# Fourier transform and gated feed-forward on one core: loads of mu behind x, tables of k1 = 0 derived later, padded weights, a short mix in one operation, a late table load

## The chip, the cores and the metric

One core of one Trainium2 chip runs the whole program. The metric is the device time of one execution in microseconds (us). A run's trace is one execution; its span, from the first to the last instruction, is about 2 us shorter than that execution's time (459.5 against 461.36 us for the kernel before). Engines are named as in the profile: PE is TensorE (matmuls), PEld its weight loads, DVE VectorE, ACT ScalarE, POOL GpSimd, SP SyncE.

## The reference

For x of 8 batches, 3072 positions and 256 features, in float32:

```python
X = np.fft.fft(np.fft.fft(x, axis=1), axis=2).real          # the real part of both transforms
x_prev = X shifted by one position (zeros in front)
xk = mu_k * X + (1 - mu_k) * x_prev
xr = mu_r * X + (1 - mu_r) * x_prev
k = relu(xk @ w_k)                                           # 256 -> 1024
out = sigmoid(xr @ w_r) * ((k * k) @ w_v)                    # 1024 -> 256
```

## The kernel before

The transform over positions is done in steps: x is multiplied with twiddles `w_pm` (96 rows), then the features are transformed with `w_eo` ("d products", into `g_all`), then 64-column matmuls with the sine tables `m1` and `m2` make the second position step ("c items", into `pq`). VectorE makes sums and differences of neighbours (`halves`, `diff`), mixes them by mu (`scaled`, `mixed`), and the k, r and v products follow. Everything is spread over one list of steps; from step 0 on, k products of one chunk run with v products of a former one. The parts that matter here:

```python
def m_rest(part):                       # after the sine and its swap, on VectorE
    s = 26 if part else 0
    if not part:                        # four 64x64 tables for feature 128
        V.tensor_copy(out=cs[lo64, 0], in_=m1[lo64, 1])
        V.tensor_copy(out=cs[hi64, 0], in_=m2[hi64, 1])
        ...                             # two more
    for m in (m1, m2):
        V.tensor_scalar(out=m[hi64, s], in0=m[hi64, s], scalar1=-1.0, ...)
        ...
            V.memset(m[hi64, 1], 0.0)
            V.tensor_copy(out=tw[:, 0 if m is m1 else 1, 0:1], in_=m[:, 0, 0:1])

def c_item(b, s0, n, eng="A"):
    ...
    if b and s0 + n == NSL:             # feature 128, once in each of batches 1 to 7
        for k in range(2):
            nc.tensor.matmul(out=ps[0:NSL, 448:512], lhsT=y_t[b, "u"][:, k],   # 27 columns
                             rhs=cs[:, k], start=(k == 0), stop=(k == 1))
    evac(pq..., eng)                    # "A": ScalarE, "V": VectorE

def v_out(c, tb, n):
    o = o_pool.tile([P, 2, 256], FP32, name="o")        # three buffers in a ring
    ...                                                 # one operation on VectorE, then two stores
        eng = nc.scalar if s and n == 1 else nc.sync

loads()                                 # SyncE: six loads of mu; GpSimd: gathers of the weights
a_sum(0, 0, 0)
a_sum(0, 0, 4)
m_sine(0, NS1)
...
m_sine(NS1, NSL)
nc.scalar.activation(out=pd_f, in_=m_pi, func=AF.Sigmoid)     # loads the sigmoid's table early
d_item(0, 3)
for lo, hi in ((0, 4), (4, 8)):         # the first two pieces of the first mixed x
    halves(0, lo + (lo > 0), hi + 1)
    diff(0, lo, hi)
    for a in range(2):
        scaled(0, 0, 0, a, lo, hi)
        mixed(0, 0, 0, a, lo, hi)
...
at(3, c_item, 0, 17, 8, "V")
```

## Time and profile before

| | before |
|---|---|
| time, median of 3 runs | 463.28 us (463.28 to 463.38) |
| the profiled execution | 461.36 us, span 459.5 |
| TensorE busy, share of the span | 450.2 us, 98% |
| first d product (record of TensorE) | 16.75 us |
| eighth group of k products starts | 38.77 us |
| from there to the end of the span | 420.7 us |

The last two rows are the ones to keep in mind. From the eighth group of k products on, the chain of waits of the kernel before has only TensorE pieces, up to the last outputs, so an execution is "when does that group start" plus "how long is the rest". (Here and below the start is that of the group's first matmul record. The chain's figure, 38.93 in the prediction, is 0.16 more, since the chain counts a piece only from the end of the one before.) The second row has a catch that I saw only later: the profiled execution was 1.9 us faster than any of the three timed ones.

### The profile page before, as it was taken

What the parts mean: (1) busy time and instruction counts of PE and PEld (TensorE: products, weight loads), DVE (VectorE), ACT (ScalarE), POOL (GpSimd) and SP (SyncE); (2) the same over time, 40 slices, a digit from 0 to 9 for tenths busy, and PEclk for the clock granted to TensorE, in tenths of its full rate; (3) what the DMA queues carried; (4) which work ended last, traced back from release to release, by engine and by line L of the source; (5) the groups of instructions that cost most, each with busy time, mean ns of one, the idle gap of its engine ahead of it and who ended that gap; (6) DMA issues with size and microseconds to landing.
All of it is one profiled execution on the core that took longest, in us unless ns stands there. A gap on an engine that the chain in (4) does not pass through costs nothing.

```text
span 459.5 us, 9810 instructions
## 1 busy us (share of the span) xinstructions
PE 450.2 (98%) x4089; PEld 329.2 (72%) x4089; DVE 361.6 (79%) x533; ACT 357.9 (78%) x397; POOL 34.9 (8%) x67
## 2 busy tenths in 40 slices
PE   8889999999999999999999999999999999999996
PEld 4657777777777777777777777777777777676765
DVE  7899978987788777978688777888679855898443
ACT  3898898788878887888878888878887888666662
POOL 8821000001000000000000000000000000000000
PEclk9999999999999999999999999999999999999999
DMA  7995462625623373324722265222222232323324
GB/s 120 147 170 100 110 137 47 139 66 119 139 47 71 56 150 95 70 58 91 165 56 65 52 138 118 69 51 66 58 60 61 56 70 47 71 59 80 70 66 95
DMA packets 32972, 40.25 MB, mean 88 GB/s; under 512 B 4480, under 2 KB 30592, under 8 KB 31584
## 3 DMA queue, kind: packets, MB, share of 16 engines
q1 hardware_dynamic: 28080, 25.07, 22.8%
q0 software_dynamic: 4688, 14.42, 18.6%
q8 instruction: 32, 0.52, 0.5%
q10 hardware_dynamic: 160, 0.13, 0.1%
q14 instruction: 12, 0.10, 0.1%
HBM read 28.84 MB, written 25.17 MB: 118 GB/s over the span
## 4 chain that ended last, share of the span: by engine, by line
PE 92%; DVE 4%; DMA 2%; issue 1%; ACT 0%; POOL 0%; SPq 0%; DVEq 0%; POOLq 0%
PE psV L573 36%; PE psW L536 35%; PE psW L559 9%; PE psW L422 4%; PE psW L398 4%; PE psW L449 3%; PE psW L412 1%; DMA xh<-in_x_dram 1%; DVE t L501 1%; DVE x L514 1%; DMA out_dram<-o 1%; DVE y L481 0%; DVE d L489 0%; DVE a L384 0%; DVE pq L384 0%
## 5 line engine op out<-in xcount | busy, mean ns | idle before, releaser
L546 ACT ACTIVATE rl<-psW 128x1024 f16<-128x1024 f32 x192 | 196.7, 1025 | 83.6 <-PE psW L536 83.6
L536 PE MATMUL psW<-x,wk 128*128 128x512 f16 (+1 forms) x776 | 197.4, 377 | 1.6 <-DVE x L514 1.3
L573 PE MATMUL psV<-wv_sb,k 128*128 128x256 f16 x1536 | 198.7, 273 | 0.0
L552 DVE TENSOR_TENSOR k<-rl 128x2048 f16<-128x2048 f16 x96 | 117.4, 1223 | 62.5 <-ACT rl L546 61.9
L573 PEld LDWEIGHTS <-k 128*128 128x128 f16 x1536 | 143.6, 98 | 20.6
L536 PEld LDWEIGHTS <-wk 128*128 128x128 f16 x776 | 75.7, 98 | 52.4 <-issue 3.1
L582 DVE SCALAR_TENSOR_TENSOR o<-psV,r 128x512 f32<-128x512 f32 (+1 forms) x97 | 66.3, 684 | 24.9 <-PE psV L573 22.4
L514 DVE TENSOR_TENSOR x<-y,t 128x1536 f16<-128x1536 f16 (+2 forms) x74 | 63.0, 851 | 2.5
L386 ACT ACTIVATE a<-psW 128x768 f16<-128x768 f32 x62 | 49.8, 807 | 4.4 <-PE psW L412 4.2
L559 PE MATMUL psW<-wr,x 128*128 128x256 f16 x384 | 49.8, 273 | 0.0
L564 ACT ACTIVATE r<-psW 128x1024 f16<-128x1024 f32 x48 | 49.0, 1021 | 0.8 <-PE psW L559 0.8
L559 PEld LDWEIGHTS <-x 128*128 128x128 f16 x384 | 37.6, 98 | 14.4 <-issue 0.2
L386 ACT ACTIVATE g_all<-psW 128x1024 f16<-128x1024 f32 (+1 forms) x47 | 47.8, 1024 | 0.0
L106 POOL DMA_DIRECT2D xh<-in_x_dram x38 | 20.0, 533 | 239.0 <-DVE eo L119 223.5
L422 PEld LDWEIGHTS <-a 128*128 128x128 f16 x384 | 25.0, 98 | 11.1 <-DVE a L384 1.0
L398 PEld LDWEIGHTS <-eo 96*128 96x128 f16 x416 | 23.4, 97 | 11.6
L119 DVE TENSOR_TENSOR eo<-xh 96x2048 f16<-96x2048 f16 x26 | 31.5, 1213 | 0.0
L422 PE MATMUL psW<-w_eo,a 128*128 128x128 f16 x376 | 28.3, 219 | 0.3 <-ACT pq L386 0.3
L386 ACT ACTIVATE pq<-psW 128x896 f16<-128x896 f32 (+5 forms) x32 | 27.6, 865 | 0.3 <-PE psW L449 0.3
L398 PE MATMUL psW<-w_pm,eo 96*128 96x96 f16 x416 | 26.3, 206 | 0.0
L449 PEld LDWEIGHTS <-g_all 128*128 128x128 f16 x459 | 17.8, 98 | 7.0 <-ACT g_all L386 0.2
L501 DVE TENSOR_SCALAR t<-d,mu_f 128x1536 f16<-128x1536 f16 (+2 forms) x42 | 22.5, 535 | 0.2
(103 smaller groups left out, 155.8 us busy)
## 6 DMA issues: line engine op xcount, KB each, us to landing
out_dram<-o SPq DMA_DIRECT2D x190, 128.0 KB, 2.4
xh<-in_x_dram POOLq DMA_DIRECT2D x28, 384.0 KB, 6.1
xh<-in_x_dram POOLq DMA_DIRECT2D x6, 192.0 KB, 6.4
wv_sb<-in_moe_w_v_dram POOLq DMA_DIRECT2D x1, 512.0 KB, 8.8
xh<-in_x_dram POOLq DMA_DIRECT2D x4, 96.0 KB, 6.9
out_dram<-o ACTq DMA_DIRECT2D x2, 64.0 KB
out_dram<-o SPq DMA_DIRECT2D x2, 64.0 KB
y<-f SPq DMA_DIRECT2D x7, 3.4 KB
```

Source lines behind the costliest of these rows:

```text
L386: nc.scalar.activation(out=out_ap, in_=in_ap, func=AF.Copy)
L398: nc.tensor.matmul(out=ps[:, 128 * i:128 * i + 96], lhsT=eo[:, 8 * j + i, e, :], rhs=w_pm[0:96, 0], start=True, stop=True)
L422: nc.tensor.matmul(out=_v(ps, 256 * i + 64 * (1 - e), [(128, 2), (1, 64)]), lhsT=a_t[b][:, e, 2 * u:2 * u + 2, :], rhs=w_eo[:, e, :], star ...
L449: nc.tensor.matmul(out=ps[:, o + 64 * i:o + 64 * i + 64], lhsT=g_all[:, u, col:col + 128], rhs=m[:, sl], start=first, stop=last)
L514: V.tensor_tensor(out=dst, in0=_v(y_t[b], 64 * (NSL * a + lo + 3 * m), [(1, n)]), in1=_v(x_t["t", a], 64 * lo, [(1, n)]), op=ALU.subtract ...
L536: nc.tensor.matmul(out=st["k", ds][:, 512 * hs + lo:512 * hs + hi], lhsT=wk_sb[m][a][:, 128 * fc:128 * fc + 128], rhs=xk[:, a, 512 * i + l ...
L546: nc.scalar.activation(out=st["rl"][:, 2 * ds:2 * ds + 2], in_=st["k", ds].rearrange("p (f t) -> p f t", f=2), func=AF.Relu, bias=0.0, sca ...
L552: V.tensor_tensor(out=k2_t[c][:, 2 * ds - 2:2 * ds + 2], in0=r, in1=r, op=ALU.mult)
L559: nc.tensor.matmul(out=ps[:, 256 * tb:256 * tb + 256], lhsT=x_t[b, 1, m][:, a, 512 * i + 128 * tb: 512 * i + 128 * tb + 128], rhs=wr_sb[m] ...
L564: nc.scalar.activation(out=st["r", c], in_=ps, func=AF.Sigmoid)
L573: nc.tensor.matmul(out=st["v"][:, 256 * h:256 * h + 256], lhsT=k2_t[c][:, fc, 128 * tb:128 * tb + 128], rhs=wv_sb[:, fc], start=(fc == 0), ...
L582: V.scalar_tensor_tensor(out=o.rearrange("p a b -> p (a b)")[:, 0:256 * n], in0=st["v"][:, 0:256 * n], scalar=16.0, in1=st["r", c][:, 256 ...
```

## The change

Its intent: get the first mixed x and the first k products earlier (x's load without the small loads of mu beside it, less table work on VectorE ahead of the first c items, a mix of one operation in place of two), make the odd matmul of feature 128 as cheap as its neighbours, and free the last output from waiting for a store.

```diff
-    cs = const.tile([P, 2, 64], FP16)
+    mz = const.tile([P, 2, 64], FP16)
+    u128 = const.tile([P, 2, 128], FP16)          # weights of feature 128, zeros in columns 27 to 127
 def m_rest(part):
-        if not part:                              # four cs operations go
-            V.tensor_copy(out=cs[lo64, 0], in_=m1[lo64, 1])
-            ...
-                V.memset(m[hi64, 1], 0.0)
-                V.tensor_copy(out=tw[:, 0 if m is m1 else 1, 0:1], in_=m[:, 0, 0:1])
+                V.tensor_copy(out=mz[lo64, n], in_=m[lo64, 1])
 def loads():
+        V.memset(mu_f, 0.0)
 def plain_128():                                  # runs in step 5
-        for n, m in enumerate((m1, m2)):
-            V.tensor_copy(out=tw[:, n, 1:NSL], in_=m[:, 1:NSL, 0])
+        V.memset(u128, 0.0)
+        V.tensor_copy(out=tw[lo64, 0, 1:NSL], in_=m1[lo64, 1:NSL, 0])
+        ...                                       # ten operations on VectorE in all
 def c_item(b, s0, n, eng="A"):
-                nc.tensor.matmul(out=ps[0:NSL, 448:512], lhsT=y_t[b, "u"][:, k],
-                                 rhs=cs[:, k], start=(k == 0), stop=(k == 1))
+                nc.tensor.matmul(out=ps[:, 448:512], lhsT=u128[:, k],
+                                 rhs=(m1, m2)[k][:, 1], start=(k == 0), stop=(k == 1))
+def mix_short(b, lo, hi):                         # d * mu + y in one operation
+        for a in range(2):
+            V.scalar_tensor_tensor(out=xo[:, a, 64 * lo:64 * hi], in0=..., scalar=mu_f[:, a, 0:1],
+                                   in1=..., op0=ALU.mult, op1=ALU.add)
 def v_out(c, tb, n):
-        o = o_pool.tile([P, 2, 256], FP32, name="o")
+        o = o_pool.tile([P, 2, 256], FP32, name="o" if n == 2 else f"o{tb}",
+                        bufs=3 if n == 2 else 1)
 ...
-    loads()
     a_sum(0, 0, 0)
 ...
     m_rest(0)
+    loads()
 ...
-    nc.scalar.activation(out=pd_f, in_=m_pi, func=AF.Sigmoid)
 ...
-    keep_busy(2)
+    d_half(0, 16, ps_v(), "A")
+    d_half(0, 18, ps_v(), "A")
 ...
-    at(2, d_item, 0, 4)
-    at(3, c_item, 0, 17, 8, "V")
+    at(3, c_item, 0, 17, 8)                       # evacuated by ScalarE
```

(Cut: the clearing of `mz`, the c items' use of it in place of `m[:, 1]`, the writing of u into `u128`, the shift of one r product by a step, and the remaining table copies.)

More of the change, by code (lines that the diff above doesn't have):

```diff
@@ L300, in m_rest @@
         s = 26 if part else 0
-        if not part:
-            V.tensor_copy(out=cs[lo64, 0], in_=m1[lo64, 1])
-            V.tensor_copy(out=cs[hi64, 0], in_=m2[hi64, 1])
-            V.tensor_copy(out=cs[hi64, 1], in_=m1[hi64, 1])
-            V.tensor_scalar(out=cs[lo64, 1], in0=m2[lo64, 1], scalar1=-1.0, scalar2=None,
-                            op0=ALU.mult)
         if part:
@@ L310, in m_rest @@
             V.tensor_copy(out=m1[hi64, 25], in_=m1[lo64, 25])
-        for m in (m1, m2):
+        for n, m in enumerate((m1, m2)):
             V.tensor_scalar(out=m[hi64, s], in0=m[hi64, s], scalar1=-1.0, scalar2=None,
@@ L337, in gather @@
                                      bass.IndirectOffsetOnAxis(ap=row_i[:, n:n + 1], axis=0))
+    V.memset(mz, 0.0)
     def loads():
+        V.memset(mu_f, 0.0)
         mus = [mu.rearrange("(a b) -> a b", b=1) for mu in (moe_mu_k, moe_mu_r)]
@@ L374, in plain_128 @@
                         scalar2=1.0, op0=ALU.mult, op1=ALU.add)
-        for n, m in enumerate((m1, m2)):
-            V.tensor_copy(out=tw[:, n, 1:NSL], in_=m[:, 1:NSL, 0])
+        V.memset(u128, 0.0)
+        V.tensor_copy(out=tw[lo64, 0, 1:NSL], in_=m1[lo64, 1:NSL, 0])
+        V.tensor_copy(out=tw[hi64, 0, 1:NSL], in_=m2[hi64, 1:NSL, 0])
+        V.tensor_copy(out=tw[hi64, 1, 1:NSL], in_=m1[hi64, 1:NSL, 0])
+        V.tensor_scalar(out=tw[lo64, 1, 1:NSL], in0=m2[lo64, 1:NSL, 0], scalar1=-1.0,
+                        scalar2=None, op0=ALU.mult)
+        V.memset(tw[hi64, :, 1:2], 0.0)
+        for n, half, sign in ((0, lo64, 1.0), (0, hi64, -1.0), (1, lo64, -1.0), (1, hi64, 1.0)):
+            V.tensor_scalar(out=tw[half, n, 0:1], in0=tw[half, n, 2:3], scalar1=sign,
+                            scalar2=None, op0=ALU.mult)
     a_t = {}
@@ L449, in c_item @@
                 nc.tensor.matmul(out=ps[:, o + 64 * i:o + 64 * i + 64],
-                                 lhsT=g_all[:, u, col:col + 128], rhs=m[:, sl],
+                                 lhsT=g_all[:, u, col:col + 128],
+                                 rhs=m[:, sl] if sl != 1 else mz[:, 0 if m is m1 else 1],
                                  start=first, stop=last)
@@ L461, in turned @@
     def turned(b):
-        y_t[b, "u"] = u = y_pool.tile([P, 2, NSL], FP16, name="u")
         for s0, n, u0, step in ((1, 24, 0, 1), (25, 2, 0, 23), (0, 1, 1, 1)):
-            V.tensor_tensor(out=u[:, :, s0:s0 + n],
+            V.tensor_tensor(out=u128[:, :, s0:s0 + n],
                             in0=_v(g_all, GU * u0 + 256, [(0, 2), (GU * step, n)]),
@@ L516, in mixed @@
                         op=ALU.subtract if m else ALU.add)
+    def mix_short(b, lo, hi):
+        x_t[b, 0, 0] = xo = x_t.get((b, 0, 0)) or mix_pool.tile([P, 2, 1536], FP16, name="x00")
+        for a in range(2):
+            V.scalar_tensor_tensor(out=xo[:, a, 64 * lo:64 * hi],
+                                   in0=_v(x_t[b], 64 * (26 * a + lo), [(1, 64 * (hi - lo))]),
+                                   scalar=mu_f[:, a, 0:1],
+                                   in1=_v(y_t[b], 64 * (NSL * a + lo), [(1, 64 * (hi - lo))]),
+                                   op0=ALU.mult, op1=ALU.add)
     def mix(b, j, m, a, lo=0, hi=24):
@@ L626 @@
         diff(0, lo, hi)
-        for a in range(2):
-            scaled(0, 0, 0, a, lo, hi)
-            mixed(0, 0, 0, a, lo, hi)
+        mix_short(0, lo, hi)
     work = {}
@@ L650 @@
     k_products(chunks[0], 1, 0, 256)
-    keep_busy(2)
+    d_half(0, 16, ps_v(), "A")
+    d_half(0, 18, ps_v(), "A")
     for n, c in enumerate(chunks):
-        at(4 * n + (5 if n == 2 else 4), r_item, c)
+        at(4 * n + (5 if n in (0, 2) else 4), r_item, c)
     at(0, m_swap, NS1, NSL)
```

## The prediction

> **What bounds the kernel now.** I read the page's shares first, then the chain that ended last in order of time, then the timeline of the first 38 us, then the windows of the DMA traffic. The page says that TensorE sets the time:
>
> ```profile
> PE 450.2 (98%) x4089; PEld 329.2 (72%) x4089; DVE 361.6 (79%) x533; ACT 357.9 (78%) x397; POOL 34.9 (8%) x67
> ...
> PE 92%; DVE 4%; DMA 2%; issue 1%; ACT 0%; POOL 0%; SPq 0%; DVEq 0%; POOLq 0%
> ```
>
> The reader should see that 8% of the chain is not TensorE, and ask where. The chain in order of time answers: all of it lies before 33 us and after 451 us. Between those, there are only PE pieces. Of the start:
>
> ```profile
> 1.90 4.70 DMA xh<-in_x_dram
> 6.60 0.14 issue
> 6.74 2.73 PE psW L412 x16
> 9.47 0.02 issue
> 9.49 0.81 ACT a L386
> 10.30 0.67 ACT m L285
> ...
> 13.84 1.19 issue
> 15.03 0.95 DVE a L384
> ...
> 33.14 1.02 PE psW L536 x4
> ```
>
> So the first x load gates TensorE, then two ACT operations, then VectorE without a break from 11.0 to 16.7 us, then VectorE again from 19.3 to 33.1. After that, only work removed from TensorE itself is worth anything. The one odd spot in that middle, which comes back in each of batches 1 to 7, is the matmul of feature 128:
>
> ```profile
> 119.38 0.35 PE psW L449 x12
> 119.72 0.16 PE psW L454 x2
> 119.89 0.98 PE psV L573 x8
> 120.87 0.86 PE psW L536 x4
> ```
>
> Twelve matmuls of 64 columns take 0.35 us (29 ns each); the two of line 454, also 64 columns, take 0.16 (80 ns each), and the eight after them 0.98, where such a group elsewhere takes 0.87. The DMA traffic at the start, in two windows (columns: PE busy, clock, DMA share, GB/s):
>
> ```profile
> 3.00:9.30 6.30, 5.62 (x25) 1.00 0.85 140
> 9.30:12.00 2.70, 2.70 (x21) 1.00 1.03 196
> ```
>
> In the first window the loads of mu, 306 packets of 4 bytes, share the engines with x. In the second they are gone, and the bytes per second are 1.4 times as many.
>
> [...] The line 454 weights have 27 columns, all others 128[...]. [...] Here the load takes 1.28 us (21.82 to 23.10) and the next ACTIVATE starts at 23.11[...]. [...] In this trace a scaling by mu of 128x256 takes 0.75 us instead of 0.30 while GpSimd issues the load of wv (20.05 to 21.03), and both end together[...].
>
> **The change, part by part.**
> (1) *Padded weights.* Per batch, the two matmuls become like the twelve: 0.16 falls to 2 x 0.029 = 0.06, and the group behind falls from 0.98 to 0.87. That is 0.10 + 0.11 = 0.21 us on the binding engine, with seven batches (14 matmuls of line 454): 7 x 0.21 = 1.5 us. Nothing else waits there, so all of it should show.
> (2) *mu behind x.* Line by line, x of batch 0 is 1.57 MB as written (the issue sizes: six of 192 KB, four of 96 KB). At 140 GB/s the 6.3 us window moved 0.88 MB; at 196 GB/s that takes 4.5. So later parts of x land up to 1.8 us sooner, the last one at 12.5 instead of the 14.3 after which the last x matmuls start (14.42). The first lands at perhaps 5.7 instead of 6.60. The filler matmuls end at 5.85 and the twiddles w_pm at 5.73, so TensorE starts about 5.9 instead of 6.74: 0.8 us. The sine (10.20) then ends before VectorE is through with its clearing at 10.11; with the new clearing of mz (0.09, as its like), VectorE starts the swap at 10.2, against 11.00: 0.8 gained.
> (3) *k1 = 0 tables.* In the first table pass VectorE drops four cs operations (11.85 to 12.50, 0.67), two clearings and two tw copies (about 2 x 0.25), and gains two mz copies (2 x 0.17) and the clearing of mu_f (0.1): about 0.8 to 0.9 less. Together with (2), the first d products start at about 15.0 instead of 16.75: 1.75 sooner. If x came no sooner, they would still start at about 15.7. The tw work comes back in step 5: ten small operations more, eight of them net of what it did before, about 1.1 us of VectorE at 35 us.
> (4) *Short mix in one operation.* A scalar_tensor_tensor of 256 elements took 0.42 us in the last output; I take the same here, 0.35 to 0.4 in a row. Two make 0.8 us where the four old ones took 1.62 (20.34 to 21.96[...]) and 1.15 (22.88 to 24.03). Saved: 0.8 and 0.35. The second half of the first mixed x is ready at 24.03 - 1.75 - 0.8 - 0.35 = 21.1.
> (5) *Order of work.* Two filler matmuls (0.43) give way to real products that were to come later. But ACT now takes an evacuation from VectorE (the c item with "V", 1.15 on VectorE, 0.92 on ACT) and splits one of 1.03 in two of 0.60. The table load leaves the start (1.28 + 0.20) and comes back before the first sigmoid (1.28).
> Between 24.6 and 31.8 us ACT already runs without a break, so I laid its list out from 20.05 (m_sine, 21.80 - 1.75) at 0.92 each: the sixth relu ends near 31.0, the table load at 32.3, the sigmoid at 33.4, two a's at 34.8, the seventh relu at 35.8. TensorE can then start the eighth group of k products at about 36.1 instead of 38.93. That is 2.8; I count 2.4, since VectorE runs at its limit there too (I get it only 2.2 ahead at the first output, with the tables of step 5 in its way).
> (6) *Own buffers for the last two outputs.* The last output operation waits 0.90 us for a store and starts at 455.77; TensorE ends at 455.41. Saved: 0.34.
> Sum: 2.4 + 1.5 + 0.3 = 4.2 us, so 463.28 - 4.2 = 459.1.
>
> **The rivals.** *ACT takes the place of VectorE at the start.* For it: no gap in its list, one evacuation more and the table load in the middle. Against it: the same list shows waits of 1.05 us to spare after 32 us before. If ACT's list is 1.5 us longer than I count, (2) to (5) give only about 1, and the time is 460.5. *mu comes too late.* Its loads start only when VectorE has cleared mu_f, about 12.0[...]. Before, the first ones took 4.3 us to land; mu is needed at 18.6 now, so there are about 2 us to spare. If all of it is used up, and 1 to 2 us more, the start gains nothing and the time is about 461. Gathers of mu landed 3.8 us after issue, which speaks against it. *The padded weights cost as much as the short ones*, because what is paid is the wait for u: then the time is 460.6. Against it, the delay also stands behind the pair, where nothing waits for u. *A better start than I count*: a full 2.9 there[...] gives 458.
>
> **Range and chances.** The middle and the end (1.8 us) I hold for likely; the start may be anything from 0.5 to 3.3. That puts eight cases in ten between 457.7 and 461.3. 2% is 9.3 us, more than twice all that I find, so faster by over 2% gets 0.02, within 2% 0.96, slower 0.02.
>
> **What would show it.** The pair in the chain at 0.06 us with 0.87 behind it, and 128-column loads. PE's first x matmul at 5.9 and the first d product near 15.0. The two short mixes of 0.4 us, without a wait for a DMA ahead of them. ACT without idle time from about 20 to 36 us, with the table load near 31 us. PE alone in the chain from 36 us on. A wait for mu_f or wk on VectorE or TensorE near 19 us, or a chain that runs through ACT or VectorE until well after 36 us, would make the prediction wrong.

## The result, and the profile after

| | before | after |
|---|---|---|
| first comparison, median | 463.33 us (463.28 to 463.89, 4 runs) | 460.64 us (459.58 to 461.76, 4 runs) |
| the same kernels later, 5 rounds | 463.43 us (37 runs) | 460.13 us (459.27 to 460.77, 6 runs) |

The ratios are 0.9939 (95% interval 0.9911 to 0.9968) and 0.9924 (0.9908 to 0.994). A ratio is the mean time of one kernel's fast runs over that of the other's of the same rounds, so it is not quite the ratio of the medians. Below I turn each ratio into microseconds against the kernel before by (ratio - 1) x 463.4: here -2.8 and -3.5, together about -3.2. The median of the first comparison, 460.64, is 1.5 us above the predicted 459.1 and inside its range.

All profiled executions are in the fast state. The page of the changed kernel, TensorE's busy time and the shares of the chain:

```profile
PE 447.2 (97%) x4087; PEld 327.6 (71%) x4087; DVE 360.0 (78%) x532; ACT 358.8 (78%) x398; POOL 35.6 (8%) x67
...
PE 93%; ACT 3%; DMA 1%; POOL 1%; issue 1%; DVE 0%; another core or an unknown queue 0%; POOLq 0%
```

TensorE lost 3.0 us of busy time, and in the chain VectorE's 4% have become ScalarE's 3%. The chain of the changed kernel in order of time (start, length, what) shows where:

```profile
4.99 6.68 DMA xh<-in_x_dram
...
11.80 2.15 PE psW L421 x24
...
20.29 1.03 ACT g_all L395
...
33.06 1.98 ACT rl L565 x2
...
35.06 1.28 ACT L583
...
36.35 1.03 ACT r L583
...
37.43 1.02 PE psW L555 x4
...
40.16 0.86 PE psW L555 x4
```

From 20.29 to 37.38 us the path runs mostly on ScalarE, for 13.6 of 17.1 us. Its last pieces are two relus, the table load (`ACT L583`, 1.28 us), and the sigmoid; only then TensorE is alone. The last line is the eighth group of k products. The pair of feature 128, in the same chain later:

```profile
120.40 0.35 PE psW L458 x12
120.75 0.06 PE psW L464 x2
120.81 0.88 PE psV L592 x8
```

The two matmuls now take 0.06 us and the eight behind them 0.88, where before they took 0.16 and 0.98. The DMA traffic in the two windows of the start (last two columns: DMA share, GB/s):

```profile
3.00:9.30 6.30, 6.19 (x36) 3.56 (x35) 5.64 (x29) 2.33 (x4) 5.95 (x16) 1.00 0.98 166
9.30:12.00 2.70, 1.41 (x15) 0.95 (x13) 2.46 (x14) 1.60 (x3) 2.27 (x6) 1.00 0.92 168
```

166 GB/s instead of 140 in the first window: x does come sooner. The short mixes on VectorE, from its timeline:

```profile
19.88 0.88 DVE L531 SCALAR_TENSOR_TENSOR x<-d,mu_f,y 128x256 f16<-128x256 f16 x2
...
21.66 0.88 DVE L531 SCALAR_TENSOR_TENSOR x<-d,mu_f,y 128x256 f16<-128x256 f16 x2
```

Two in 0.88 us, and no wait in brackets ahead of them: mu is there in time.

Then the surprise. The eighth group starts at 40.00 us by TensorE's record, *later* than the 38.77 of the page before, and yet the kernel is faster by its timed runs (the two traced executions are equally long, 459.5 us each). The reason is that the page before was a lucky execution. A repeated run of the kernel before (463.15 us, an ordinary execution) has this in its timeline (idle time before, and its releaser, in brackets):

```profile
15.88 0.81 ACT L386 ACTIVATE a<-psW 128x768 f16<-128x768 f32 x1 [1.81 <-PE psV L412]
...
17.15 1.01 PE L142 MATMUL psV<-zeros 128*128 128x512 f16 x2 [2.70 <-ACT a L386]
```

The eight last x matmuls begin at 13.63 and their records take 0.82 us, but ScalarE gets on only at 15.88. TensorE then stands idle for 2.70 us, which the page before did not show. The eighth group of this execution starts at 40.55. All comparisons below are therefore with this trace, not with the page before.

### The profile page after: what moved, and what is told of

The parts are those of the page before. It is cut to its first block, busy times and chain, and to the rows that moved or that the text cites. A ratio compares the mean times of both kernels' runs of the same rounds, so it can differ in the third digit from the quotient of the medians.

```text
span 459.5 us, 9804 instructions
## 1 busy us (share of the span) xinstructions
PE 447.2 (97%) x4087; PEld 327.6 (71%) x4087; DVE 360.0 (78%) x532; ACT 358.8 (78%) x398; POOL 35.6 (8%) x67
## 4 chain that ended last, share of the span: by engine, by line
PE 93%; ACT 3%; DMA 1%; POOL 1%; issue 1%; DVE 0%; another core or an unknown queue 0%; POOLq 0%
PE psV L592 36%; PE psW L555 35%; PE psW L578 9%; PE psW L431 5%; PE psW L407 4%; PE psW L458 3%; DMA xh<-in_x_dram 1%; ACT rl L565 1%; ACT g_all L395 1%; PE psW L421 1%; POOL xh L106 1%; ACT a L395 0%; ACT L583 0%; ACT pq L395 0%; ACT m L287 0%
## 5 line engine op out<-in xcount | busy, mean ns | idle before, releaser
L523 DVE TENSOR_TENSOR x<-y,t 128x1536 f16<-128x1536 f16 (+1 forms) x70 | 61.8, 882 | 2.4
L583 ACT ACTIVATE r<-psW 128x1024 f16<-128x1024 f32 x48 | 49.0, 1021 | 0.8 <-PE psW L578 0.8
L395 ACT ACTIVATE pq<-psW 128x896 f16<-128x896 f32 (+5 forms) x33 | 28.7, 871 | 1.6 <-PE psW L431 1.1
L510 DVE TENSOR_SCALAR t<-d,mu_f 128x1536 f16<-128x1536 f16 (+1 forms) x38 | 20.6, 543 | 0.1
```

The lines of the kernel that those rows point to most:

```text
L395: nc.scalar.activation(out=out_ap, in_=in_ap, func=AF.Copy)
L523: V.tensor_tensor(out=dst, in0=_v(y_t[b], 64 * (NSL * a + lo + 3 * m), [(1, n)]), in1=_v(x_t["t", a], 64 * lo, [(1, n)]), op=ALU.subtract ...
L583: nc.scalar.activation(out=st["r", c], in_=ps, func=AF.Sigmoid)
```

## The experiments

Twelve runs, each timed over five rounds against the kernel before on the same chip. They went to three chips: b0, a0, b_pad and b_tail to one, b_mu, b_tab, a_muearly and a_tail2 to the next, the other four to a third. The changed kernel as it is was timed on the first of these and in the comparison above, so its edited versions are compared with it through the kernel before. From the spread of the single times such a difference is good to about 0.9 us (95%). In the diffs, "before" and "changed" name the kernel that was edited. This table holds what the single verdicts rest on. The time is turned from the ratio as above; "first d" and "eighth group" are starts in TensorE's record of the one traced execution; "rest" is from the eighth group to the end of the span.

| run | us against before | first d | eighth group | rest |
|---|---|---|---|---|
| b0: before, unchanged | +0.3 | 17.96 | 40.55 | 420.70 |
| b_pad: before + padded weights | -1.5 | 17.95 | 40.57 | 419.25 |
| b_tail: before + own output buffers | +0.4 | 18.28 | 40.80 | 420.96 |
| b_mu: before + loads of mu behind x | -0.4 | 17.25 | 40.31 | 420.71 |
| b_tab: before + k1 = 0 tables | +0.5 | 15.99 | 40.88 | 421.22 |
| b_mutab: before + both of these | -0.9 | 15.09 | 39.60 | 421.22 |
| a0: changed, again | -3.5 | 15.36 | 39.02 | 419.48 |
| a_muearly: changed, loads of mu in front | -2.1 | 17.67 | 41.61 | 419.49 |
| a_mixlong: changed, short mix in two | -2.4 | 15.13 | 39.23 | 419.48 |
| a_sig: changed, sigmoid's table early | -4.1 | 14.77 | 37.17 | 419.52 |
| a_tail2: changed, some stores moved | -4.6 | 15.05 | 38.19 | 418.92 |
| a_tail2_c17v: that, c item back on VectorE | -3.2 | 16.07 | 40.42 | 419.78 |

(The first trace of the changed kernel: 15.65, 40.00, 419.49.)

"Rest" hardly moves between executions: 420.70 and 420.71 in two kernels, 419.48 to 419.52 in four. It carries a verdict by itself. "Eighth group" is one execution and moves by a microsecond between the two traces of the changed kernel, so there the verdict is with the times.

**b0 and a0: the same kernels again**

> The kernel before once more, unchanged, as a control and for a second trace of it: 463.3 us, ratio 1.000 within 0.001. The trace that the prediction was read from belongs to an execution of 461.4 us, 1.9 faster than its timed runs. If the spread comes from the start, this trace shows the eighth group of k products later than 38.93 us; if it comes from the middle, it shows pieces other than TensorE in the chain after 36 us.

> The changed kernel once more, for a second trace and a narrower interval: 460.6 us, between 459.5 and 461.8. If the late TensorE signals of the first trace (24 to 28 us) are an accident of that execution, this trace doesn't have them and its start is 1 to 2 us shorter; if they belong to the kernel, it has them too.

b0: median 463.43 us (463.15 to 464.73, 14 runs), ratio 1.0006 (0.9997 to 1.0015). a0: 460.13, given above. Two equal kernels thus came out 0.3 us apart. b0's later eighth group (40.55) puts the spread at the start, the first of its two cases: the trace of the kernel before that I had predicted from is not its usual execution. And the late signals of TensorE that a0's text asks about belong to the changed kernel: ScalarE waits for one ahead of `pq` for 1.11 us at 27.29 in the first trace and for 1.01 at 26.84 in a0, whose start is 1.0 us shorter all the same.

The granted clock adds to it. Two windows of b0 (PE busy first, the granted clock third from the end):

```profile
13.80:17.20 3.40, 0.70 (x9) 0.55 (x8) 1.92 (x6) 1.49 (x3) 3.10 (x4) 0.96 0.65 108
17.20:19.70 2.50, 2.50 (x19) 1.95 (x19) 1.34 (x3) 0.82 (x2) 1.89 (x3) 0.50 0.97 154
```

After a stretch in which TensorE is busy for 0.70 of 3.40 us, the clock falls to half (0.50), and the d products at 17.96 take 107 ns each, against 57 in the page before (eight from 16.75 to 17.21, at a clock of 1.00). The half-clock stretch of b0 is 3.41 us long by the trace's clock record, that of b_pad 6.83. From 13.54 to 16.95, ahead of b0's, TensorE has 0.91 us of matmul records. But this stretch isn't what makes the ordinary executions slow: b_tail's trace has no such stretch (the clock is 1.00 from 16 to 20 us) and its eighth group starts at 40.80 all the same. The changed kernel had none in both of its traces; b_tab, b_mutab and a_muearly have one between 27.8 and 33.3 us.

**b_pad: padded weights alone**

```diff
 # before
+    u128 = const.tile([P, 2, 128], FP16)               # zeroed once; u is written into it
-                nc.tensor.matmul(out=ps[0:NSL, 448:512], lhsT=y_t[b, "u"][:, k],
+                nc.tensor.matmul(out=ps[:, 448:512], lhsT=u128[:, k],
```

> The kernel before with only the weights of feature 128 padded to 128 columns. [...] pair of 0.06 us in the chain, 0.87 behind it, 7 x 0.21 = 1.5 us less, 461.8. If the delay is the wait for u on VectorE: no change, 463.3.

Median 462.02 us (460.93 to 462.67, 8 runs), ratio 0.9967 (0.9954 to 0.998): -1.5 us. The rest after the eighth group falls from 420.70 to 419.25, which is 1.45. The start is where it was (40.57 against 40.55). This part does what was said, all of it on the path, and the rival of a wait for u falls. That the width of the weights costs is shown; by what it costs is not, as no run here tells one effect of the width from another.

**b_tail: own buffers for the last two outputs alone**

```diff
 # before
-        o = o_pool.tile([P, 2, 256], FP32, name="o")
+        o = o_pool.tile([P, 2, 256], FP32, name="o" if n == 2 else f"o{tb}",
+                        bufs=3 if n == 2 else 1)
```

> The kernel before with only the own buffers for the last two outputs. By the prediction 0.34 us less, 463.0. By the trace of the changed kernel the SyncE queue, whose last three issues follow each other without a gap, sets the end: then 463.3, unchanged, though the last output operation starts earlier.

Median 463.75 us (462.98 to 465.22, 22 runs), ratio 1.0008 (1.0001 to 1.0016): +0.4, not -0.34. The last output operation on VectorE, first in b0, then in b_tail:

```profile
457.55 0.42 DVE L582 SCALAR_TENSOR_TENSOR o<-psV,r 128x256 f32<-128x256 f32 x1 [0.90 <-DMA out_dram<-o]
```

```profile
457.47 0.42 DVE L583 SCALAR_TENSOR_TENSOR o<-psV,r 128x256 f32<-128x256 f32 x1 [0.57 <-PE psV L573]
```

The wait for the store is gone, as meant: measured from the end of TensorE's last matmul the operation comes 0.34 us sooner. But the rest is 0.27 longer. What ends the program is the issue of stores. In SyncE's record the last ones stand one behind the other, 0.55 to 0.8 us each, and the last of all is issued at 458.26 for 0.55 us in b0, at 458.53 for 0.79 in b_tail. VectorE's operation had ended 0.29 and 0.64 us earlier, at 457.97 and 457.89. Counted from the end of TensorE's last matmul (457.18 and 457.44), the last issue ends 1.63 us later in b0 and 1.88 in b_tail. The buffer was not the last thing that the store waited for; SyncE's queue was. Why the last issues are longer in b_tail I have not found out.

**a_tail2: stores of the last full output tile on ScalarE's queue**

```diff
 # changed
-            eng = nc.scalar if s and n == 1 else nc.sync
+            eng = nc.scalar if s and (n == 1 or (c == chunks[-1] and tb == 1)) else nc.sync
```

> The changed kernel with half of the stores of the last full output tile issued on ACT's queue instead of SyncE's. If SyncE's issues, one after the other, set the end: its last issue starts 0.6 us sooner, at the end of the last output operation, and the time falls by 0.4 to 0.6 us to about 459.8. If the landing of the last bytes sets it: unchanged.

Median 458.97 us (458.71 to 459.31, 4 runs), ratio 0.9901 (0.9886 to 0.9917). The rest falls from 419.48 to 418.92, so 0.56 us is the tail, as expected. The times fall by 1.1 to 1.8, more than that. Its start was also the second earliest (38.19), and nothing in the edit explains this; with four runs I count only the 0.56 as shown. What is saved is time for issuing: the last issue ends 1.43 us behind the last output operation in the first trace of the changed kernel (457.04 against 455.61, on SyncE) and 0.67 us behind it here (454.47 against 453.80, on ScalarE). At the end of this program that is on the path.

**b_mu and b_tab: the two parts of the start, each alone**

```diff
 # b_mu: before
+        V.memset(mu_f, 0.0)              # in loads()
-    loads()                              # in front
+    loads()                              # behind m_rest(0)
 # b_tab: before
-    the four cs tables, two clearings and two tw copies of m_rest(0)
+    two mz copies there, and the ten operations of plain_128 in step 5 (weights still 27 columns)
```

> The kernel before with only the loads of mu held back behind the first table pass. Theory (mu's 4-byte packets slow x, and the x loads gate the start): first x matmul at 5.9 instead of 6.75 us, last x landing about 0.9 to 1.4 sooner, time 0.8 to 1 us less, 462.5. Rival (VectorE's own work sets the start, x is hidden behind it): 463.4, unchanged, although x lands sooner.

> The kernel before with only the new tables: no cs, feature 128 from the tables of k1 = 0, its weights left at 27 columns. VectorE's first table pass is shorter by 0.8 us. Theory of the prediction (VectorE sets the start from 11 to 16.7 us): up to 0.8 us less, 462.6. Rival (in the usual execution the d products wait for the last x matmuls, whose signals come near 16 us, and not for VectorE): 463.4, unchanged.

b_mu: 463.22 us (463.12 to 463.48, 13 runs), ratio 0.9991 (0.9983 to 0.9999), -0.4. b_tab: 464.21 us (462.75 to 465.02, 21 runs), ratio 1.001 (1.0003 to 1.0017), +0.5. The d products do start sooner, by 0.7 and 2.0 us against b0, but next to nothing of it arrives at the end. x comes sooner in b_mu: from 3.00 to 9.30 us its trace has 163 GB/s, against 140 in the page before, and its first x matmul starts at 5.85 instead of 6.74. b_mu lies between its two cases; that b_tab is slower was in neither of its own. Where b_tab's lead goes is seen in the next run, which has the same two losses.

**b_mutab: both together**

```diff
 # before: both edits above
```

> The kernel before with two parts together: the loads of mu behind x and the tables of k1 = 0 (weights of feature 128 still 27 columns, all else as before). Alone, the first part gave 0.4 us and the second lost about 0.5. Theory 'both are needed': the d products start when the last of x and VectorE's table pass are both there, so taking one away leaves the other; together they should give 1 to 2 us: 461.5 to 462.5. Rival 'they add up': -0.4 + 0.5, about 463.5, the same as before. The trace should show the first d products at 15.0 to 16.0 us in the first theory.

Median 462.75 us (one of 14 runs, at 951 us, is left out as slow), ratio 0.998 (0.9972 to 0.9989): -0.9. Together they give more than their sum of +0.1, so the first theory stands in direction; in size it is below the expected 1 to 2. Two things take some of it back. The first is a wait of ScalarE for a signal of TensorE, and then of TensorE for ScalarE (its timeline):

```profile
26.88 1.02 ACT L392 ACTIVATE pq<-psW 128x1024 f16<-128x1024 f32 x1 [1.90 <-PE psW L428]
...
27.95 1.01 PE L428 MATMUL psW<-w_eo,a 128*128 128x128 f16 x8 [2.31 <-ACT pq L392]
```

The matmuls of this `pq` end at 24.07 by their records. The third group of k products was 3.4 us ahead of b0's (24.12 against 27.54), the fourth is only 1.1 ahead (30.10 against 31.19). In b_tab the two waits are 2.41 and 2.61 us. All traces with the new tables but a_sig's have ScalarE wait there, for 1.0 to 2.4 us; b0 has no such wait there. Why the signal comes late is not shown. The second is in the chain:

```profile
38.77 0.15 DVE tw L371
...
40.22 1.22 DVE k L559
...
42.47 0.44 DVE x L521
...
42.95 0.94 PE psW L566 x7
```

The table work taken away at 12 us comes back at 38.77 and holds VectorE for 1.45 us. A square of k and a mixed x stand behind it, and TensorE's r products at 42.95 wait for that x. It shows in the rest too: 421.22 in both kernels that have the tables but not the rest of the change, 420.70 without, so 0.5 us is paid after the eighth group.

**a_muearly: the changed kernel with the loads of mu in front**

```diff
 # changed
-        V.memset(mu_f, 0.0)
+    loads()                              # in front again
```

> The changed kernel with the loads of mu at the front again, all else kept. Theory: first x matmul at 6.75, the start 0.8 to 1 us longer, 461.0 against 460.1 to 460.6. Rival (x is hidden): 460.3, unchanged.

Median 461.96 us (459.35 to 463.14, 9 runs), ratio 0.9954 (0.9934 to 0.9974): a loss of 0.7 to 1.4 us against the two comparisons of the changed kernel. Its last x matmuls start at 14.72, against 13.49 in a0, and its first d product at 17.67 against 15.36. So the same part that is worth 0.4 us in the kernel before is worth about 1 here, where VectorE no longer hides it; from b_tab to b_mutab it is worth 1.4. The late eighth group of this trace (41.61) is not all due to mu: the clock is at half from 29.90 to 33.31, and a group of k products on the chain there takes 1.72 us in place of 1.02. The times do not rest on that alone: the five of its runs with a mean clock of 0.997 or more have a mean of 461.0 us, the five of a0 with 0.998 or more 459.9.

**a_mixlong: the changed kernel with the short mix in two operations**

```diff
 # changed
-        mix_short(0, lo, hi)
+        for a in range(2):
+            scaled(0, 0, 0, a, lo, hi)
+            mixed(0, 0, 0, a, lo, hi)
```

> The changed kernel with the short mix again in two operations (scaling by mu, then the sum) for each of the four pieces. If VectorE's list carries the start, as my step 4 had it, this loses 0.8 to 1.15 us: 461.2 to 461.6 beside 460.1 to 460.6 of the changed kernel. If ScalarE's list carries it, as the chains of its traces show from about 20 us on, VectorE has that much to spare and it loses nothing: 460.1 to 460.6.

Median 461.08 us (460.29 to 461.80 in 5 runs; one at 2675 us is left out as slow), ratio 0.9948 (0.9934 to 0.9962): a loss of 0.4 to 1.1 us, about 0.7. This is not clear of the noise: the interval overlaps with both of the changed kernel (0.9911 to 0.9968 and 0.9908 to 0.994). Nor does the trace settle it. The third group of k products starts at 24.15, against 24.96 in a0, and the eighth, at 39.23, between those of the two traces of the changed kernel. So a loss is likely, but it is not shown, and of the two theories neither falls.

**a_sig: the changed kernel with the sigmoid's table loaded early**

```diff
 # changed
     m_sine(NS1, NSL)
+    nc.scalar.activation(out=pd_f, in_=m_pi, func=AF.Sigmoid)
     d_item(0, 3)
```

> The changed kernel with the sigmoid's table loaded early again, by the same small activation in the same place as in the kernel before. ScalarE then pays 1.28 + 0.20 us near 20 us and no longer 1.28 near 34. If ScalarE's list has no gap between the two places, the order doesn't matter: within 0.4 us of the changed kernel. If there are gaps ahead of 24 us that can take it, the time falls by up to 1.3: 459. If the early place delays the evacuations that the first mixed x needs, it loses up to 1.5: 462.

Median 459.04 us (458.46 to 460.56, 6 runs), ratio 0.9911 (0.9897 to 0.9925): a gain of 0.6 to 1.3 us over the changed kernel, good to the 0.9 us said above and so only just clear of the noise. The second of the outcomes expected, gaps that take the load, is the one that fits. ScalarE's timeline in a0 and then in a_sig:

```profile
22.00 1.02 ACT L395 ACTIVATE g_all<-psW 128x1024 f16<-128x1024 f32 x1
...
26.84 1.02 ACT L395 ACTIVATE pq<-psW 128x1024 f16<-128x1024 f32 x1 [1.01 <-PE psW L431]
...
34.08 1.28 ACT L583 ACT_TABLE_LOAD   x1
35.38 1.02 ACT L583 ACTIVATE r<-psW 128x1024 f16<-128x1024 f32 x1
```

```profile
20.29 1.28 ACT L642 ACT_TABLE_LOAD   x1
21.59 0.20 ACT L642 ACTIVATE pd_f<-m_pi 128x1 f32<-128x1 f32 x1
21.70 1.01 ACT L395 ACTIVATE g_all<-psW 128x1024 f16<-128x1024 f32 x1
...
25.40 1.02 ACT L395 ACTIVATE pq<-psW 128x1024 f16<-128x1024 f32 x1
...
31.03 1.98 ACT L565 ACTIVATE rl<-psW 128x1024 f16<-128x1024 f32 x2
32.84 1.09 ACT L583 ACTIVATE r<-psW 128x1024 f16<-128x1024 f32 x1
```

At the late place there is no slack: in a0 the load fills the whole time between the relus that end at 34.06 and the sigmoid at 35.38, and TensorE's seventh group of k products, at 36.45, waits for that sigmoid. In a_sig the sigmoid follows the relus at once. Which slack takes the load at the early place is not shown. It has to lie behind that place; a0 has such a gap, the 1.01 us ahead of `pq`. But the execution of a_sig was already 1.8 us ahead when its load came (the `g_all` that starts at 19.93 in a0 starts at 18.10), after the same operations, and its `pq` waits for nothing. So the difference between the two traces is partly that of two executions, and the worth of this part is taken from the times.

**a_tail2_c17v: the c item's evacuation given back to VectorE**

```diff
 # a_tail2
-    at(3, c_item, 0, 17, 8)
+    at(3, c_item, 0, 17, 8, "V")
```

> The best kernel so far (changed, with half of the last full output tile's stores on ScalarE's queue, 458.97) and the evacuation of the c item that the change took from VectorE given back to it: ScalarE 0.92 us less, VectorE 1.15 more. If ScalarE's list carries the start, it gains 0.5 to 0.9: 458.1 to 458.5. If VectorE is as close to its limit, nothing, or a loss of up to 0.5: 459.0 to 459.5.

Median 460.73 us (459.27 to 461.97, 6 runs), ratio 0.9931 (0.9918 to 0.9945): a loss of 1.4 us against a_tail2, more than the 0.5 expected at most. As a_tail2's own time is 0.5 to 1.2 us lower than its edit explains, the firm part of this is what the rest shows, 0.86 (below). VectorE was the nearer limit, so this part of the change is right. The chain of this run has VectorE in the lead up to 44 us:

```profile
33.59 1.13 DVE pq L393
...
41.39 1.22 DVE k L571
...
43.64 0.44 DVE x L523
...
44.12 0.94 PE psW L578 x7
```

The evacuation is the first line. It pushes the tables of step 5 and all behind them back, and TensorE's r products wait for the mixed x as in b_mutab; the rest is 0.86 us longer than a_tail2's. So the tables could be moved to step 5 without this loss only because the same change took this evacuation from VectorE there.

**The sum of the parts.** Padded weights -1.5, mu and tables together -0.9, short mix -0.7, evacuation on ScalarE -1.4, late table load +1.0 (the middle of 0.6 to 1.3), own buffers +0.3: -3.2, as measured. The parts were taken from different kernels, the short mix is not clear of the noise, and with the 0.86 of the rest for the evacuation the sum is -2.7, so the agreement is partly luck. The best kernel that I ran is a_tail2 with 458.97 us, not to be told from a_sig with 459.04; a_tail2 with the early table load was not tried.

## Why the prediction was right, and where its sizes were off

It predicted -4.2 us; the runs gave -2.8 and -3.5. By its own steps:

1. *Padded weights, 1.5 us.* Right: 1.5 in time, 1.45 in the rest, 0.06 and 0.88 in the chain.
2. *mu behind x.* Right at the place: the first x matmul came at 5.85 (predicted 5.9), mu was not waited for. But the last part of x landed at 13.43 by the trace's record, not 12.5. Without mu the first window moved 166 GB/s, not the 196 that the prediction took from the second, and the second window now moved 168; so mu's packets account for 26 of the 56 GB/s at most. The swap's gain (10.2 against 11.0) existed only against the page before; in b0 it starts at 10.14 already.
3. *k1 = 0 tables.* The first d products came at 15.65 and 15.36 for the predicted 15.0. The return of the work in step 5 was priced at 1.1 us and took 1.45 in b_mutab; it was harmless only thanks to step 5's other part.
4. *Short mix, 0.8 + 0.35.* The operation took 0.44 us for the predicted 0.4. Its worth is about 0.7, if that is more than noise, and less than 1.15. The lengthened scaling of the page before (0.75 us in place of 0.30) was not there in an ordinary execution: the first scaling in b0's chain, at 22.42, takes 0.29. That alone leaves 0.7 of the 1.15. That it ran beside GpSimd's issue of the load of wv (20.05 to 21.03) does not show the cause: an operation of 0.30 us that had waited for the end of that issue would end near 21.33, and it ended at 21.09.
5. *Order and ScalarE's list: the eighth group at 36.1, 2.4 us counted for the start.* This is the term that was mis-sized most. The group started at 40.00 and 39.02 in the two traces. The sixth relu was to end near 31.0 and the table load at 32.3; the load began at 35.06. ScalarE's list began 1.3 us later than laid out (its `g_all` at 20.29, the sine at 21.32 for the predicted 20.05), it had gaps of 1.11 and 0.41 us ahead of 29 us, the first of them the late signal of TensorE, and the load of 1.28 stood in it with nothing to hide behind. The late beginning and the gaps make 2.8 of the 4.0 us by which the sixth relu ended late (35.04 for 31.0); the other 1.2 are a list longer than laid out. I had treated the moved load as neutral; by a_sig's times it costs about 1.
6. *Own buffers, 0.34.* Failed: 0.27 the other way, because SyncE's issue of the stores sets the end.

So the rest after the eighth group was to fall by 1.5 + 0.34 = 1.84 and fell by 420.70 - 419.49 = 1.21. The start was to give 2.4. Taking 1.21 off the times leaves 1.6 and 2.3 for it. That it came so near 2.4, with an eighth group 3 to 4 us later than laid out, is two errors that cancel: the list was too short, and the reference point, 38.77 of the page, was 1.8 us ahead of the ordinary 40.55. The rival *ScalarE takes the place of VectorE at the start*, put at 460.5, describes the result best: the chain of the changed kernel is mostly ScalarE's from 20 to 37 us, and the times are 460.64 and 460.13. "PE alone from 36 us on" came at 37.43 and, in a0, at 36.45.

What stays open is why the ordinary executions of the kernel before lose 2 us near 14 to 17 us. b0, b_pad, b_tail and b_mu show it, all kernels with the k1 = 0 tables are without a gap of that length, but these are single traces. The traces show late releases behind the last x matmuls, not their cause. The kernels with these tables have one near 25 to 28 us instead (b_mutab above), and its cause is as open.

## What to carry to other kernels

Before a prediction counts from a place in a profile, compare the profiled execution's own time with the timed ones; here it was 1.9 us faster, as much as the start was to gain. Work that is moved costs what the new place has no slack for, so look at the idle time of that engine behind both places: the table load went to a place on the chain where ScalarE had none, and the tables of step 5 fitted only because an evacuation left. A removed wait is worth something only if nothing else, here the issue of the stores, ends at the same time.

## What the traces show of the hardware

- Two matmuls with 27-column weights among 128-column ones cost 0.10 us more themselves (0.16 against 0.06) and 0.10 to 0.11 in the group behind (0.98 against 0.88 and 0.87): 1.45 us for seven pairs in b_pad's rest.
- The load of the sigmoid's table takes 1.28 us (21.82 to 23.10 in the page before). It begins 0.02 us after the operation ahead of it (35.04 to 35.06 in the changed kernel), and the next activation starts 0.01 to 0.02 us after it (36.34 to 36.35 there, 21.57 to 21.59 in a_sig).
- In the tail, issues of 64 and 128 KB stores take 0.55 to 0.80 us each on SyncE, and moving some of them to ScalarE's queue shortened the rest by 0.56 us.
- Some releases come late, and no trace here shows why. Behind the last x matmuls of b0 the records end at 14.45 (13.63 + 0.82) and ScalarE is released at 15.88, 1.4 us later; behind the c item of b_mutab they end at 24.07, and ScalarE, free from 24.98, starts at 26.88.
